# Block 0 of the first MLP in two pieces for its first two column groups: 480 tokens of five attention tiles, then the 32 of the sixth

## The chip, the cores and the metric

One core of one Trainium2 chip runs the whole program. The metric is the device time of one execution in microseconds, the median of three runs. Engines are called TensorE (PE, with its weight loads PEld), VectorE (DVE), ScalarE (ACT), GpSimd (POOL) and SyncE (SP, which here only issues transfers).

## The reference

Chunked attention over 4 batches, 8 heads, 768 positions, 64 dimensions: each chunk of 32 queries sees 8 memory positions and the keys from 16 before to 8 behind the chunk. Its output, 3072 tokens of 512, goes through two MLPs:

```python
x = attention(q, k, v, mem_k, mem_v)             # 3072 x 512
gate = 1.0 / (1.0 + np.exp(-(x @ w_gate)))       # 512 x 1536
x = gate * (x @ w_val) @ w_out                   # 1536 x 512
h = x @ w_in                                     # 512 x 2048
return (h * sigmoid(1.702 * h)) @ w_out2         # 2048 x 512
```

Weights arrive as 64-bit floats.

## The kernel before

**Tiles and blocks.** Attention is worked out in 32 tiles of 96 tokens (`TQ`), the MLPs in 6 blocks of 512 tokens (`BLK`). Block 0 is therefore tiles 0 to 4 and the first 32 tokens of tile 5; the other 64 tokens of tile 5 belong to block 1. Tiles 0 to 5 are the prologue (`NPRO` = 6) with buffers of their own; tiles 6 to 8 use one set of buffers in turn, and both kinds are transposed on PE. The tiles from 9 on are transposed on DVE, from keys and queries that SP loads in many small pieces into the buffers in which weights were converted before.

**One prologue tile** (`attention`, line 362) goes so: loads of q, k, v and memory on SP; transposes of q and k on PE (L406, L414), evicted by ACT (L421, L426, L427); scores on PE (L525); maximum and subtraction on DVE (L542, L545), exponential on ACT (L553), sum and reciprocal on DVE (L587, L589, L590); normalization on DVE and POOL (L598); transposes of the probabilities on PE (L620), evicted by ACT (L627); product with v on PE (L676); and the split of the result into a high part (ACT, L722) and a low part (DVE, L725), xh and xl, which the MLP multiplies. Tile 5's split is in two pieces, one for each block; the second, `evict(1)`, is held back and also needs the key `x1`: the buffers of block 1's xh and xl serve first as raw buffers for the weights value 1 and out 0.

**Banks.** PSUM has 8 banks: G, V, A0, A1 and Y0 to Y3. All prologue tiles use Y0 and Y1 for transposed q and k, A0 and A1 for scores, Y2 and Y3 for transposed probabilities, and G for the product with v. In the first MLP G and V take the gate and value products, Y0 to Y3 the output product.

**Weights** are turned from 64 bits into a high and a low part in 36 conversions, in the order gate 0, value 0, gate 1, value 1, out 0, gate 2, value 2, out 1, gate 3, ... (number = column group of 128 of the 1536). Each is a load on SP (L268), then on ACT L272, on DVE L277, a sign step on DVE (L286) or ACT (L282) in turn, a join on DVE (L291), the high part on ACT (L296), and the low part (L301) on DVE for two of three, on POOL for the third. From the ninth conversion on they need buffers, and from the tenth slots, of a pool that opens (`open_late`) when the prologue's buffers are given back, the last by tile 5.

**First MLP** (lines 1019 to 1038). For each block and each of the 12 column groups: the gate product (`first_product`: eight multiplies with the weight's high part, L784, four with its low part, L791), tanh on ACT (L808), the value product, the gating tail (DVE L811, ACT L816, DVE L819), and then the output product `gemm2` of the column group before (twelve multiplies, L975). `SPLIT` already cuts block 1 into two halves of 256 tokens for its first ten column groups.

**The order.** Every step is a task with an engine, an estimated duration and a due time. `Schedule.run` hands due times back from products to what they need, and then gives each engine, whenever it is free in the plan, the task with the earliest due time among those that are ready in the plan. The order of each engine is thus fixed when the program is built, and the engine follows it, whatever comes late. The products' due times come from a running `clock` that begins at 34 and adds 1.12 times each product's estimate. A prologue tile's last split is due at 34 less 2 us for each tile that comes after it among the six.

When PE would be idle before the first product, the plan puts in multiplies with an identity (`sch.fill`, L848) that write bank V.

Of the kernel before, what the change touches and what calls it, by code (L numbers as in the profile page):

```python
# [22 lines left out]
TQ = CH * NCK  # L23
# [100 lines left out]
def c_dve(n, k=1):  # L124
    return k * 0.13 + n / 960.0


def c_act(n):
    return 0.13 + n / 1200.0
# [7 lines left out]
def kernel(  # L137
# [30 lines left out]
    BLK = 512  # L168
# [4 lines left out]
    NPRO = len(tiles[0])  # L173
# [4 lines left out]
    clock = [34.0]  # L178
# [9 lines left out]
    G, V, A0, A1 = 0, 1, 2, 3  # L188
    Y = [4, 5, 6, 7]
# [129 lines left out]
    def dma(dst, src, key, r=(), act=False, dur=0.45):  # L319
        n = 8  # L320
        for d in src.shape:
            n *= d
        q_ = nc.scalar if act else nc.sync
        add("act" if act else "sp", dur, lambda: q_.dma_start(out=dst(), in_=src), r=list(r), w=[key], nbytes=n)
# [30 lines left out]
    STEP = 2.0  # L355
# [6 lines left out]
    def attention(t, bufs, banks, pe_path, extra=None, nth=0, last=False):  # L362
# [9 lines left out]
        def tadd(eng, dur, fn, r=(), w=(), more=0.0, **kw):  # L372
            add(eng, dur, fn, r=r, w=w, slack=SL + more, **kw)
# [310 lines left out]
        def evict(part=None):  # L684

            g = range(t * NCK, (t + 1) * NCK)
            for i, blk in enumerate(sorted({c // NCH for c in g})):
                if part not in (None, i):
                    continue
                cs = [c for c in g if c // NCH == blk]  # L690
                a = (cs[0] - g[0]) * CH
                m = len(cs) * CH
                x0 = cs[0] % NCH * CH
                xb = blk % 2
                if blk >= NB - 2:
                    for bk, kb, c0, p0, n in outs:
                        src = bk[:, c0 : c0 + n * TQ].rearrange("p (a s) -> p a s", a=n)[:, :, a : a + m]
                        dst = T["qt"][:, p0 : p0 + n, :m]
                        tadd("act", c_act(n * m), lambda d=dst, s=src: nc.scalar.activation(d, s, AF.Copy), r=[kb], w=[kk["qt"]])
                    o = (blk - NB + 2) * BLK + x0  # L700
                    dma(
                        lambda o=o, m=m: x_dram.rearrange("(a p) c -> p a c", p=P)[:, :, o : o + m],
                        T["qt"][:, :, :m],
                        ("xd", blk, t),
                        r=[kk["qt"]],
                        act=True,
                    )
                    continue
                due = None
                if t < NPRO and blk == 0:  # L710
                    due = clock[0] - STEP * (NPRO - 1 - t)
                elif t < NPE and blk <= 1 and SPREAD:

                    due = clock[0] + SPREAD * (t - NPRO + 1) / (NPE - NPRO)
                for o, (bk, kb, c0, p0, n) in enumerate(outs):
                    src = bk[:, c0 : c0 + n * TQ].rearrange("p (a s) -> p a s", a=n)[:, :, a : a + m]
                    at = (slice(None), slice(p0, p0 + n), slice(x0, x0 + m))
                    wx = [("x", xb, c % NCH, e) for c in cs for e in (range(2) if pe_path else (o,))]
                    rx = [kb] + (["x1"] if xb else [])

                    def ev_xh(src=src, at=at, xb=xb):
                        nc.scalar.activation(xhs[xb][at], src, AF.Copy)  # L722

                    def ev_xl(src=src, at=at, xb=xb):
                        nc.vector.tensor_tensor(  # L725
                            out=xls[xb][at], in0=src, in1=xhs[xb][at].bitcast(F32), op=ALU.subtract
                        )

                    tadd("act", c_act(n * m), ev_xh, r=rx, w=wx)
                    tadd("dve", c_dve(n * m), ev_xl, r=rx, w=wx, due=due)  # L730

        rp = kvn + [(kk["pt"], 0), (kk["pt"], 1)]
        if pe_path:
            tadd("pe", 0.8, pe_pv, r=rp, w=[kbv], margin=mg)
            if t < NPRO - 1 or t >= NPRO:
                evict()
            else:

                evict(0)
                held_back.append(lambda: evict(1))  # L740
        else:
            late.append(dict(pv=pe_pv, rp=rp, evict=evict, rest=rest))
            if last:
                for x in list(late):
                    if x is not late[0]:
                        x["rest"]()
                    tadd("pe", 0.9, x["pv"], r=x["rp"], w=[kb0, kb1])
                    x["evict"]()
                late.clear()
# [94 lines left out]
    pro = pro_stack.enter_context(tc.tile_pool(name="pro", bufs=1))  # L844
    ident = {"pro": pro.tile([P, P], F32, tag="ident", name="ident")}
    make_identity(nc, ident["pro"])
    pro_banks = [(Y[0], Y[1], A0, A1, Y[2], Y[3], G)] * NPRO
    sch.fill = lambda: nc.tensor.matmul(bank[V][:, :P], ident["pro"], ident["pro"], start=True, stop=True)  # L848
    pro_bufs = []
    for i in range(NPRO):  # L850
# [163 lines left out]
    TT = BLK // P  # L1014

    LOAD = 1.12
    SPLIT = {1: (10, BLK//2)}
    pend = None
    for b in range(NB - 2):
        n = BLK  # L1020
# [4 lines left out]
        steps = [(f, 0, n) for f in range(F1)]  # L1025
        if b in SPLIT:
            lead, c1 = SPLIT[b]
            steps[:lead] = [(f, c, m) for c, m in ((0, c1), (c1, n - c1)) for f in range(lead)]
# [538 lines left out]
```

## Time and profile before

| | before |
|---|---|
| median of 3 runs | 1166.68 us (1166.3 to 1166.88) |
| profiled execution | 1167.84 us, of it the span 1166.0 us |
| PE busy | 1150.3 us (99%) |
| DVE busy | 770.5 us (66%) |
| ACT busy | 531.1 us (46%) |
| mean granted clock of PE | 0.997 |

The span runs from the first to the last instruction of the profiled execution; its own time has 1.84 us more around it. Busy time of PE is no measure of its pace, because multiplies overlap each other; the starts of neighbouring multiplies show the pace. In rows in order of time the first column is the start, the second how long the row lasts, and what stands in brackets is the idle time ahead of it and what ended that. `x4` is four instructions in one row.

### The profile page before, as it was taken

What the parts mean: (1) busy time and instruction counts of PE and PEld (TensorE: products, weight loads), DVE (VectorE), ACT (ScalarE), POOL (GpSimd) and SP (SyncE); (2) the same over time, 40 slices, a digit from 0 to 9 for tenths busy, and PEclk for the clock granted to TensorE, in tenths of its full rate; (3) what the DMA queues carried; (4) which work ended last, traced back from release to release, by engine and by line L of the source; (5) the groups of instructions that cost most, each with busy time, mean ns of one, the idle gap of its engine ahead of it and who ended that gap; (6) DMA issues with size and microseconds to landing.
All of it is one profiled execution on the core that took longest, in us unless ns stands there. A gap on an engine that the chain in (4) does not pass through costs nothing.

```text
span 1166.0 us, 19472 instructions
## 1 busy us (share of the span) xinstructions
PE 1150.3 (99%) x7288; PEld 959.8 (82%) x7288; DVE 770.5 (66%) x1460; ACT 531.1 (46%) x953; POOL 129.1 (11%) x150
## 2 busy tenths in 40 slices
PE   8899999999999999999999999999999999999998
PEld 7788899987888888888888878888888888888886
DVE  7899657877677777888866978867244365343332
ACT  6778622223222323676545766655243353233332
POOL 5333233112222111000000001000000000000000
PEclk9899999999999999999999999999999999999999
DMA  9756244234444524344327645574233452244001
GB/s 215 218 183 198 76 106 99 51 82 115 86 95 89 118 55 119 111 169 154 108 65 225 212 166 187 174 251 123 69 121 114 126 163 82 84 123 120 27 37 36
DMA packets 211070, 144.40 MB, mean 124 GB/s; under 512 B 146208, under 2 KB 166944, under 8 KB 210976
## 3 DMA queue, kind: packets, MB, share of 16 engines
q1 hardware_dynamic: 177048, 128.74, 39.0%
q10 hardware_dynamic: 33928, 14.42, 4.5%
q8 instruction: 57, 0.93, 0.4%
q14 instruction: 37, 0.30, 0.1%
HBM read 107.45 MB, written 35.65 MB: 123 GB/s over the span
## 4 chain that ended last, share of the span: by engine, by line
PE 96%; DVE 2%; ACT 1%; DMA 0%; POOL 0%; issue 0%; SPq 0%; DVEq 0%; POOLq 0%
PE bank L1321 29%; PE bank L758 22%; PE bank L975 17%; PE bank L784 15%; PE bank L791 8%; PE bank L676 2%; PE bank L525 2%; DVE pw L598 0%; DVE sm L587 0%; DMA qn<-in_q_dram 0%; DVE e L545 0%; DVE mx L542 0%; DVE xl L725 0%; PE bank L620 0%; PE bank L414 0%; DMA vn<-in_v_dram 0%
## 5 line engine op out<-in xcount | busy, mean ns | idle before, releaser
L1321 PE MATMUL bank<-sb_x,sb_r 128*128 128x512 f32 x1512 | 362.5, 389 | 0.4 <-ACT sb_s L1333 0.4
L1321 PEld LDWEIGHTS bank<-sb_x,sb_r 128*128 128x128 f32 x1512 | 283.7, 188 | 60.0 <-ACT sb_s L1333 1.1
L758 PE MATMUL bank<-w,gh 128*128 128x512 f32 x624 | 192.1, 389 | 0.0
L784 PE MATMUL bank<-xh,w 128*128 128x512 f32 (+1 forms) x464 | 160.7, 358 | 2.7 <-DVE xl L725 1.4
L784 PE MATMUL bank<-xl,w 128*128 128x512 f32 (+1 forms) x464 | 159.5, 355 | 0.5 <-DVE xl L725 0.5
L975 PE MATMUL bank<-gh,w 128*128 128x512 f32 (+1 forms) x656 | 157.3, 365 | 0.0
L758 PEld LDWEIGHTS bank<-w,gh 128*128 128x128 f32 x624 | 117.2, 188 | 24.2
L975 PEld LDWEIGHTS bank<-gh,w 128*128 128x128 f32 x656 | 114.6, 189 | 20.1 <-ACT gh L1348 0.3
L758 PE MATMUL bank<-w,gl 128*128 128x512 f32 x312 | 121.4, 389 | 0.0
L1337 DVE TENSOR_TENSOR sb_s<-bank,sb_s 128x512 f32<-128x512 f32 x108 | 74.3, 690 | 70.6 <-PE bank L1321 58.7
L791 PE MATMUL bank<-xh,w 128*128 128x512 f32 (+1 forms) x464 | 107.5, 356 | 0.0
L1333 ACT ACTIVATE sb_s<-bank 128x512 f32<-128x512 f32 x108 | 65.0, 602 | 84.3 <-PE bank L1321 78.7
L784 PEld LDWEIGHTS bank<-xh,w 128*128 128x128 f32 x464 | 88.4, 190 | 16.5 <-ACT sig L808 2.0
L784 PEld LDWEIGHTS bank<-xl,w 128*128 128x128 f32 x464 | 88.5, 191 | 13.1 <-DVE xl L725 1.0
L791 PEld LDWEIGHTS bank<-xh,w 128*128 128x128 f32 x464 | 78.1, 189 | 12.7
L642 DVE STREAM_TRANSPOSE pt<-raw 32x256 f32<-32x256 f32 x184 | 79.7, 433 | 5.0 <-PE bank L676 1.9
L975 PE MATMUL bank<-gl,w 128*128 128x512 f32 (+1 forms) x328 | 80.3, 367 | 0.0
L808 ACT ACTIVATE sig<-bank 128x512 f32<-128x512 f32 (+1 forms) x58 | 30.6, 528 | 89.6 <-PE bank L791 79.8
L1364 ACT ACTIVATE sig<-sb_s 128x512 f32<-128x512 f32 x72 | 45.4, 632 | 57.0 <-DVE sb_s L1337 36.0
L758 PEld LDWEIGHTS bank<-w,gl 128*128 128x128 f32 x312 | 58.6, 188 | 12.3
L301 POOL TENSOR_TENSOR w<-f,w 128x512 fp32r<-128x512 f32 x17 | 27.3, 1603 | 355.4 <-ACT w L296 355.3
L816 ACT ACTIVATE gh<-sig 128x512 fp32r<-128x512 f32 (+1 forms) x58 | 32.4, 558 | 73.2 <-DVE sig L811 69.1
(161 smaller groups left out, 1494.0 us busy)
## 6 DMA issues: line engine op xcount, KB each, us to landing
sb_r<-wc_dram SPq DMA_DIRECT2D x133, 256.0 KB
raw<-in_moe_w_out_dram SPq DMA_DIRECT2D x24, 512.0 KB
raw<-in_moe_w_in_dram SPq DMA_DIRECT2D x16, 512.0 KB
wc_dram<-sb_r SPq DMA_DIRECT2D x15, 512.0 KB
wf_dram<-f SPq DMA_DIRECT2D x24, 256.0 KB
y_dram<-f ACTq DMA_DIRECT2D x24, 256.0 KB
raw<-wf_dram SPq DMA_DIRECT2D x24, 256.0 KB
out_dram<-f SPq DMA_DIRECT2D x23, 256.0 KB
```

The source lines that it names most:

```text
L301: eng.tensor_tensor(out=w[:, 1, :], in0=ft, in1=w[:, 0, :].bitcast(F32), op=ALU.subtract)
L642: nc.vector.transpose(T["pt"][r * CH : (r + 1) * CH, :, c * CH : (c + 1) * CH], T["pn"][c * CH : (c + 1) * CH, :, kb * CH : (kb + 1) * CH],)
L758: nc.tensor.matmul(ps_out, a, c, start=(first and i == 0 and j == 0), stop=(last and i == n - 1 and j == 2),)
L784: nc.tensor.matmul(bank[bk][:, :n], w[:, 0, ts[t]], x[xb][:, t, c0 : c0 + n], start=t == 0 and x is xhs, stop=False)
L791: nc.tensor.matmul(bank[bk][:, :n], w[:, 1, ts[t]], xhs[xb][:, t, c0 : c0 + n], start=False, stop=t == NK - 1)
L808: nc.scalar.activation(sig[:, :n], bank[src_sig][:, :n], AF.Tanh, scale=scale / 2)
L816: nc.scalar.activation(gh[:, :n], sig[:, :n], AF.Copy, scale=0.5)
L975: nc.tensor.matmul(bank[into[m]][:, c0 : c0 + n], w[:, wi, m * P : (m + 1) * P], g[:, :n], start=f == 0 and j == 0 and c0 == 0, stop=f == ...
L1321: nc.tensor.matmul(bank[bk], w[:, o : o + P], xt[x, k][:, xl, :], start=first and k == 0 and wl == 0 and xl == 0, stop=k == 1 and wl == 1, ...
L1333: add("act", c_act(BLK), lambda: nc.scalar.activation(work[n], bank[bk], AF.Copy), r=[("bank", bk)], w=[n])
L1337: nc.vector.tensor_tensor(out=work[n], in0=bank[bk], in1=work[n], op=ALU.add)
L1364: add("act", c_act(BLK), lambda: nc.scalar.activation(sigs[i], src(), AF.Tanh, scale=0.851), r=[ksrc], w=[ks])
```

## The change

The first two column groups of block 0 are multiplied in two pieces, with columns 0 to 479 first for both and then columns 480 to 511 for both; the output products of these pieces are cut in the same way. Tiles 0 to 4 are due 2 us apart with tile 4 at the start of the clock (each 2 us later than before), and tile 5 has no due time of its own any more: it has that of the first product that reads its 32 tokens, and of those that write its banks. Tile 5's product with v goes to bank A0 in place of G.

```diff
                 due = None
                 if t < NPRO and blk == 0:
-                    due = clock[0] - STEP * (NPRO - 1 - t)
+                    due = clock[0] - STEP * (NPRO - 2 - t) if t < NPRO - 1 else None
...
-    pro_banks = [(Y[0], Y[1], A0, A1, Y[2], Y[3], G)] * NPRO
+    pro_banks = [(Y[0], Y[1], A0, A1, Y[2], Y[3], G)] * (NPRO - 1) + [(Y[0], Y[1], A0, A1, Y[2], Y[3], A0)]
...
-    SPLIT = {1: (10, BLK//2)}
+    SPLIT = {0: (2, 5 * TQ), 1: (10, BLK // 2)}
```

By the plan's clock the first product that reads tile 5 is due at 47.6, after four products of 480 tokens (2.72 each) and one output product of 480 tokens (2.72).

## Rows read from the trace of the kernel before

**Rows 1.** Stretches: stretch, length, busy time per engine, granted clock, DMA share, GB/s

```profile
30.00:35.00 5.00, 2.76 (x33) 2.29 (x31) 5.00 (x12) 3.78 (x6) 3.50 (x2) 1.00 0.68 209
35.00:40.00 5.00, 3.55 (x31) 3.14 (x32) 4.42 (x11) 4.37 (x9) 1.49 (x3) 0.65 0.08 21
```

**Rows 2.** All engines in order of time, around the first product

```profile
34.13 0.54 DVE L725 TENSOR_TENSOR xl<-bank,xh 128x384 fp32r<-128x384 f32 x1
...
38.25 0.37 SPq L268 DMA_DIRECT2D raw_s<-in_moe_w_gate_dram  x1
...
38.74 0.62 DVE L725 TENSOR_TENSOR xl<-bank,xh 128x256 fp32r<-128x256 f32 x2 [0.27 <-ACT xh L722]
...
39.51 0.76 PE L784 MATMUL bank<-xh,w 128*128 128x512 f32 x1 [1.40 <-DVE xl L725]
...
43.44 0.40 PE L784 MATMUL bank<-xl,w 128*128 128x512 f32 x1
```

**Rows 3.** PE in order of time, at the beginning of block 2

```profile
268.30 0.50 PE L784 MATMUL bank<-xl,w 128*128 128x512 f32 x1 [0.53 <-DVE xl L725]
```

**Rows 4.** All engines in order of time, tiles 4 and 5

```profile
25.49 0.73 DVE L542 TENSOR_REDUCE mx<-bank 96x4 f32<-96x256 f32 x2
...
26.22 0.74 DVE L545 TENSOR_TENSOR e<-bank,mx 96x256 f32<-96x256 f32 x2
...
27.76 1.78 DVE L598 TENSOR_TENSOR pw<-e,sm 32x448 f32<-32x448 f32 x2
...
30.25 0.87 ACT L627 ACTIVATE pt<-bank 128x384 f32<-128x384 f32 x2 [0.41 <-PE bank L620]
...
32.98 0.47 ACT L722 ACTIVATE xh<-bank 128x384 fp32r<-128x384 f32 x1
```

**Rows 5.** DVE in order of time, the first gating

```profile
47.16 0.69 DVE L811 SCALAR_TENSOR_TENSOR sig<-sig,bank 128x512 f32<-128x512 f32 x1 [2.94 <-PE bank L791]
```

**Rows 6.** PE in order of time: tile 6, output product 0, gate 3

```profile
46.88 0.60 PE L414 MATMUL bank<-ident_a,qkn_a 128*128 128x128 f32 x4
47.23 0.48 PE L784 MATMUL bank<-xh,w 128*128 128x512 f32 x1
...
52.81 1.07 PE L975 MATMUL bank<-gh,w 128*128 128x512 f32 x4
...
64.07 0.39 PE L784 MATMUL bank<-xh,w 128*128 128x512 f32 x1
```

**Rows 7.** Groups of DVE instructions from 20 to 47 us: busy us, mean ns

```profile
L598 DVE TENSOR_TENSOR pw<-e,sm 32x448 f32<-32x448 f32 (+1 forms) x6 | 5.1, 877 | 0.0
...
L291 DVE SCALAR_TENSOR_TENSOR f<-f,raw 128x512 int32<-128x512 int32 x4 | 2.7, 673 | 0.0
L301 DVE TENSOR_TENSOR w<-f,w 128x512 fp32r<-128x512 f32 x4 | 2.7, 694 | 0.0
L587 DVE TENSOR_REDUCE sm<-e 96x8 f32<-96x512 f32 x3 | 2.0, 672 | 0.6 <-ACT e L553 0.6
L277 DVE TENSOR_SCALAR raw<-raw 128x512 int32<-128x512 int32 x4 | 1.5, 408 | 0.0
L286 DVE TENSOR_SCALAR raw<-raw 128x512 uint16<-128x512 uint16 x2 | 1.5, 741 | 0.0
```

**Rows 8.** PE in order of time: 512 columns, 256 columns, product with v

```profile
140.76 0.40 PE L784 MATMUL bank<-xh,w 128*128 128x512 f32 x1
...
142.58 0.28 PE L784 MATMUL bank<-xh,w 128*128 128x256 f32 x1
...
143.41 0.28 PE L784 MATMUL bank<-xl,w 128*128 128x256 f32 x1
143.62 0.88 PE L676 MATMUL bank<-pt,vn 128*64 128x96 f32 x16
```

**Rows 9.** Waits of DVE from 43 to 136 us: total, times, longest

```profile
DVE sig L811 <- PE bank L791: 5.1, 4, 2.9
```

**Rows 10.** ACT in order of time: the high part of gate 3

```profile
50.19 0.63 ACT L296 ACTIVATE w<-f 128x512 fp32r<-128x512 f32 x1
```

**Rows 11.** SP in order of time: the first small loads

```profile
134.16 0.80 SPq L324 DMA_DIRECT2D f<-in_q_dram  x2
```

## Prediction

> **What bounds the kernel now.** I read the stretches first, then the instructions in order of time around the first product of the first MLP, then groups and waits of VectorE (DVE), and last the place where block 2 begins. TensorE (PE) does not run well until 43.44 us: the first product starts at 39.51 and its first nine multiplies take 3.93 us, while from 43.44 on they come every 0.23 us; the stretch 35 to 40 shows a granted clock of 0.65 [rows 1, 2]. From there to the end PE is busy nearly everywhere; its waits after 140 us are few, and one of them, 0.53 us at 268.30, matters below [rows 3]. So the end moves with the moment at which PE has its stream, unless a later stage takes it back.
>
> Why 39.51? The first product reads all 512 tokens of block 0, and its bank G is also the bank in which tile 5's last product lies until both of its pieces have been split. The last low part of x is written at 38.74 (two pieces: 32 tokens of block 0 and 64 of block 1), and PE follows, while tile 4's low part is begun at 34.13 [rows 2]. The second piece waits for the buffer of x1, that is for value 1 and out 0 to be out of the raw buffers, which is why these two go through DVE before value 0 and gate 1. DVE is the engine that this stage is made of: from 30 to 35 it has no gap [rows 1], filled by tiles 3, 4, 5 and the first weights [rows 4], and its first long idle time is before 47.16, where it waits 2.9 us for PE [rows 5].
>
> **Part 1, a start without tile 5.** Between tile 3 and tile 4's normalization DVE does tile 5's two maxima and two subtractions, at 25.49 and 26.22, 1.4 us together; tile 4's normalization then starts at 27.76 and ends at 29.54 [rows 4]. With tile 5 due 13.6 us of plan later, these fall behind, and the normalization ends near 28.2. From its end to tile 4's high part of x at 32.98 it took 3.4 us (transposes, two evictions from 30.25, the product with v) [rows 4]; high and low part add about 1 us. 28.2 + 3.4 + 1.0 = 32.6: the first product can start about 7 us earlier. Its weight's low part is a DVE instruction that fits into the 3.4 us. On the queues tile 5's five loads on SyncE (SP) fall behind those of value 0 and gate 1, which so come earlier; its normalizations on GpSimd (POOL), its evictions on ScalarE (ACT) and its transposes on PE fall behind what is due for the first product, and no engine does more for it than before. Bank G is no reason to wait any more, since tile 5 now ends in A0. That bank's next user is tile 6, whose transposes there had not been needed for block 1 until long after; nothing near it waits, so I cost it at nothing, as long as tile 6 stays outside block 0.
>
> **Part 2, what the start then waits for.** PE needs four 480-token products, 48 multiplies of 0.214 us (Part 3), 10.3 us, before it comes to the first out product; that began at 52.81 before [rows 6]. But the out product writes the Y banks, through which tile 5's queries, keys and probabilities pass, so tile 5 must have left them. Its due time protects it, yet DVE has to do all of this by then, by the means of its groups [rows 7]:
> - value 0: 0.41 + 0.67 + 0.69 = 1.8; gate 1: 0.41 + 0.74 + 0.67 = 1.8; value 1: 1.8; out 0: 0.41 + 0.74 + 0.67 + 0.69 = 2.5;
> - tile 5: 0.7 + 0.7 [rows 4], sum 0.67, normalization 2 x 0.88: 3.9;
> - gating of column group 0: two of 0.69 [rows 5] = 1.4.
>
> Together 13.2 us. Between 28.2 and 32.6 DVE has some 4.4 us, of which gate 0 (0.74 + 0.67 + 0.69) and tile 4's low part (0.5) take 2.6; so 11.4 us are left at 32.6, and they end at 44.0. After tile 5's normalization come its eight transposes and two evictions, as in tile 4 about 2 us: 46.0 for the first out product, against 42.9 if PE were the limit. ACT and the weight loads have as much to do but are idle more often in these stretches, so I charge nothing for them; if a load comes late, the cover is gone and the 46.0 moves by as much. Bounds: 44.0 with no tail, 48.5 if the tail is twice as long. PE's clock before 46.0 costs nothing extra, because DVE sets that time; a lower clock would only fill the wait.
>
> **Part 3, the small pieces.** Two column groups, gate and value of 12 multiplies each: 48 pieces of 32 columns; the two out products add 24: 72 more multiplies, with as many columns in all. The trace has no such multiply. Eight of 512 columns take 1.82 us from the first's start to the next kind's (0.2275 each), and of 256 columns the first and the eighth start 0.83 us apart (0.1186) [rows 8]; the line through the two, 0.000425 a column, gives 0.024 at 32 columns, the lower end. The upper end is the shortest full-height multiply that is seen alone, a 128x128 transpose, four in 0.35 us, 0.088 each [rows 6]. In between lies the product with v, 128 rows by 96 columns: sixteen in 0.88 us with the drain of the last, 0.055 each [rows 8]. I take 0.05, the nearest in columns. 72 x 0.05 = 3.6 us after the out product's start, less 24 x 0.0136 (32 columns on that line) = 0.3 because the out products' large pieces are shorter, plus 0.35 for the transposes of tile 6 at 46.88, which lay ahead of it before and will lie behind. That is 3.6 (ends: 1.8 and 6.3). ACT and DVE get four small instructions each, beside other work: a 512-column gating takes 0.69 [rows 5], so they are cheap while these engines wait for PE.
>
> A rule weighs against this part. The Trainium skill, TensorE: Matmul & The Clock Gate, section "Wait — 56ns, not 53.3ns?", gives a floor of about 62 ns per MATMUL when its decoding is done in microcode; an estimate by it is 72 x 0.062 = 4.5 instead of 3.6, and 0.9 us more in the end. The row with 0.055 is below that floor.
>
> **The sum.** 52.81 - 46.0 = 6.8 earlier, less 3.6: 3.2 us gained. The profiled execution took 1167.84 (span 1166.0 and 1.8 around it), so 1164.6 against it; the runs' median is 1166.68, so 1163.5.
>
> **Does it last?** DVE must deliver the remaining weights 3.2 us earlier too. Up to 136 us PE never waits for a weight, while DVE waits for PE in four gatings, 5.1 us in all [rows 9]; that idle time moves out, DVE follows PE. Gate 3's high part is written at 50.19 and multiplied at 64.07: 13 us to spare [rows 6, 10]. Block 2 is the tighter point: PE stands 0.53 us there for the low part of x [rows 3], and the attention tiles of that stage hang on SP's queue of small loads, which begins at 134.16, when the converting buffers come free [rows 11], and goes on issuing up to there. If DVE finishes the weights 3 us earlier, the queue starts so much earlier.
>
> **The rivals.**
> - *Given back at block 2* (0.15): the queue of small loads does not start earlier, and PE waits at 268 for what it had won. For: the 0.53 us show that there is no spare. Against: the 5.1 us of DVE waiting for PE. Time: 1166.2 to 1167, no change.
> - *A larger gain* (0.12): DVE interleaves so well that PE is the limit, the out product at 42.9, small pieces at the lower end: 9.9 - 1.8 = 8.1, which gives 1158.6, or 1161 if half of the difference to the forecast is lost.
> - *Slower by the late pool* (0.13): buffers and identity of the next stage open when tile 5's product with v is done, by 38.25 now; the load of gate 3 goes out then and stands at the head of SP's in-order queue until then, with value 3, tile 6 and later weights behind it [rows 2]. From load to high part took 12.6 us (50.8 - 38.25), so it decides when the pool opens after 64.07 - 12.6 = 51.5; each us beyond is lost. Tile 5 put last everywhere, with POOL slow on its normalization, could reach 55: 1170. Against: the first out product needs tile 5 out of the Y banks by then.
> - *The start does not move* (0.10): PE's order is fixed beforehand; if the plan sees tile 5's probabilities ready before the first product, they stand ahead of it and PE waits for them as now, to about 38.25. Gain 1.3, small pieces 2.6 net (72 x 0.036): 1168.0.
>
> **How the numbers follow.** The forecast case has 0.50, within 1161.5 to 1165.5. A measurement here tells 0.2%, 2.3 us: faster means under 1164.35, slower over 1169.0. Of the forecast case 0.38 is faster, 0.12 within; the larger gain adds 0.12 faster, the loss at block 2 0.15 same, the late pool 0.13 slower, the unmoved start 0.06 same and 0.04 slower. Faster 0.50, same 0.33, slower 0.17. By the terms' ends the forecast case could reach 1159.7 (52.81 - 44.0 less 1.8) and 1168.7 (52.81 - 48.5 less 6.3); with the rivals the range 1160.2 to 1168.3 leaves out most of the late pool and half of the larger gain.
>
> **What would show it.** Right: first product at 31 to 34 with 480 columns; tile 5's low part of x after it; first out product near 46; 32-column multiplies spaced about 0.05; the queue of small loads starting near 131; block 2 near 265. Wrong: the first product behind tile 5's product with v; a PE wait ahead of the first out product that is not DVE's; PE waits over 1 us for gate 3 or at block 2; spacing above 0.09.

## The result, and the profile after

The kernel is slower: 1175.87 us (median of four runs, 1173.48 to 1177.34) against 1166.49, a ratio of 1.0078 (1.0058 to 1.0098). The profiled execution took 1177.34, of it the span 1175.5; the span grew by 9.5 us, and PE's records by 10.2 us of busy time (1160.5 against 1150.3). Where the 9.5 us stand can be read off places that PE passes in both traces:

| PE begins | before | after | difference |
|---|---|---|---|
| the first product | 39.51 | 35.45 | -4.06 |
| the first out product | 52.81 | 48.39 | -4.42 |
| block 1 | 142.58 | 149.73 | +7.15 |
| the second MLP | 487.42 | 497.1 | +9.7 |
| end of the span | 1166.0 | 1175.5 | +9.5 |

So part of the start is won; 11.6 us are lost between the first out product and block 1, 2.5 more before the second MLP, and nothing after that. PE in order of time in the kernel after:

```profile
35.45 0.48 PE L784 MATMUL bank<-xh,w 128*128 128x480 f32 x1 [0.57 <-DVE xl L725]
...
42.34 0.38 PE L784 MATMUL bank<-xl,w 128*128 128x480 f32 x1
43.16 0.88 PE L620 MATMUL bank<-ident,pw 96*128 96x96 f32 x8 [0.43 <-POOL pw L598]
43.82 1.11 PE L791 MATMUL bank<-xh,w 128*128 128x480 f32 x4
...
46.60 0.88 PE L676 MATMUL bank<-pt,vn 128*64 128x96 f32 x16
47.41 1.14 PE L791 MATMUL bank<-xh,w 128*128 128x480 f32 x4
...
49.25 0.18 PE L784 MATMUL bank<-xh,w 128*128 128x32 f32 x1
49.28 0.26 PE L784 MATMUL bank<-xl,w 128*128 128x32 f32 x1
...
49.95 0.26 PE L784 MATMUL bank<-xl,w 128*128 128x32 f32 x1
50.06 1.12 PE L975 MATMUL bank<-gh,w 128*128 128x480 f32 x4
...
58.42 0.60 PE L975 MATMUL bank<-gh,w 128*128 128x32 f32 x4
58.87 0.60 PE L791 MATMUL bank<-xh,w 128*128 128x32 f32 x4
59.32 0.61 PE L975 MATMUL bank<-gh,w 128*128 128x32 f32 x4
59.77 1.01 PE L975 MATMUL bank<-gl,w 128*128 128x32 f32 x4
60.62 0.77 PE L784 MATMUL bank<-xh,w 128*128 128x512 f32 x1
61.20 0.63 PE L784 MATMUL bank<-xl,w 128*128 128x512 f32 x1
...
66.31 0.52 PE L784 MATMUL bank<-xl,w 128*128 128x512 f32 x1
66.68 0.39 PE L784 MATMUL bank<-xh,w 128*128 128x512 f32 x1
...
149.73 0.28 PE L784 MATMUL bank<-xh,w 128*128 128x256 f32 x1
```

**The start.** Against the row at 39.51 of [rows 2] the first product is 4.06 earlier, 480 columns wide, and its multiplies come at full pace at once, where before the first nine took 3.93 us. Tile 5's transposes and product with v (43.16, 46.60), which stood ahead of the start before, now stand among the first four products.

**The small pieces.** From 49.28 to 49.95 six multiplies of 32 columns follow each other: 0.67 / 6 = 0.1117 us from start to start. Four take 0.45 at 58.42, at 58.87 and at 59.32, so 0.1125 each, whatever they multiply. The first of a series comes sooner (49.25 to 49.28), but the large pieces around it give that back: from 49.25 to 60.62 there are 60 small multiplies and 20 of 480 columns; 11.37 us less 20 x 0.2155 and less 0.4 for the last row, which runs at half pace, leaves 0.111 for each of the 60. An eighth of the columns of a 256-column multiply costs 0.94 of its time (0.1186, [rows 8]).

**The clock.** At 60.62 begin multiplies of 512 columns that come every 0.426 us from 61.20 to 66.31, against 0.2275 in [rows 8]: fourteen take 6.06 us in place of 3.19, and 59.77 takes 0.85 in place of 0.45, 3.3 us in all. The stretches say why (columns as in [rows 1]):

```profile
50.00:55.00 5.00, 5.00 (x33) 4.58 (x34) 2.24 (x6) 2.13 (x6) 1.29 (x1) 1.00 0.93 255
55.00:60.00 5.00, 5.00 (x41) 4.83 (x39) 2.14 (x6) 1.77 (x5) 1.27 (x1) 0.98 0.91 290
60.00:65.00 5.00, 5.00 (x14) 4.07 (x15) 3.86 (x9) 2.50 (x4) 0.00 (x0) 0.50 0.68 241
65.00:70.00 5.00, 5.00 (x26) 4.15 (x24) 0.74 (x2) 1.55 (x3) 0.00 (x0) 0.84 0.42 147
```

The granted clock is 0.50 from 60 to 65, the lower of PE's two levels, right behind the stretch of small pieces. PE shows 5.00 of 5 busy in all four rows, and its weight loads 4.83 in the second: neither figure gives the loss away, only the clock and the starts do.

**Later.** From block 1 to the second MLP PE stands still for longer: 3.2 us against 1.7, which is 1.5 of the 2.5 us lost there; the rest is not assigned. The waits of PE from 138 to 500 us in the kernel after (total, times, longest):

```profile
PE bank L784 <- DVE sig L811: 2.3, 2, 1.3
PE bank L784 <- ACT sig L808: 0.9, 2, 0.5
```

Before, they were two for `sig` (ACT) of 1.2 us and one for the low part of x of 0.5 [rows 3].

### The profile page after: what moved, and what is told of

It reads as the page before. It is cut to its first block, busy times and chain, and to the rows that moved or that the text cites. A ratio compares the mean times of both kernels' runs of the same rounds, so it can differ in the third digit from the quotient of the medians.

```text
span 1175.5 us, 19627 instructions
## 1 busy us (share of the span) xinstructions
PE 1160.5 (99%) x7358; PEld 968.7 (82%) x7358; DVE 769.5 (65%) x1464; ACT 532.3 (45%) x957; POOL 128.2 (11%) x150
## 4 chain that ended last, share of the span: by engine, by line
PE 90%; SPq 3%; DMA 2%; DVE 1%; issue 0%; POOL 0%; ACT 0%; DVEq 0%; POOLq 0%
PE bank L1321 29%; PE bank L758 22%; PE bank L975 15%; PE bank L784 13%; PE bank L791 7%; SPq L324 3%; PE bank L676 2%; PE bank L525 1%; DMA f<-in_q_dram 1%; DMA vn<-in_v_dram 1%; DMA raw<-in_k_dram 0%; PE bank L620 0%; DVE pt L642 0%; DMA wf_dram<-f 0%; POOL f L1009 0%
## 5 line engine op out<-in xcount | busy, mean ns | idle before, releaser
L784 PE MATMUL bank<-xh,w 128*128 128x512 f32 (+3 forms) x480 | 165.1, 356 | 3.8 <-DVE sig L811 2.3
L784 PE MATMUL bank<-xl,w 128*128 128x512 f32 (+3 forms) x480 | 163.7, 353 | 0.0
L975 PE MATMUL bank<-gh,w 128*128 128x512 f32 (+3 forms) x672 | 160.2, 363 | 0.0
L791 PE MATMUL bank<-xh,w 128*128 128x512 f32 (+3 forms) x480 | 109.7, 353 | 0.0
L784 PEld LDWEIGHTS bank<-xh,w 128*128 128x128 f32 x480 | 91.9, 191 | 18.6 <-DVE sig L811 3.2
L784 PEld LDWEIGHTS bank<-xl,w 128*128 128x128 f32 x480 | 91.8, 191 | 12.4 <-DVE xl L725 0.3
L791 PEld LDWEIGHTS bank<-xh,w 128*128 128x128 f32 x480 | 80.1, 189 | 12.4
L975 PE MATMUL bank<-gl,w 128*128 128x512 f32 (+3 forms) x336 | 81.9, 366 | 0.0
L816 ACT ACTIVATE gh<-sig 128x512 fp32r<-128x512 f32 (+3 forms) x60 | 32.7, 545 | 84.8 <-DVE sig L811 72.3
L808 ACT ACTIVATE sig<-bank 128x512 f32<-128x512 f32 (+3 forms) x60 | 30.8, 513 | 81.2 <-PE bank L791 70.2
L975 PEld LDWEIGHTS bank<-gl,w 128*128 128x128 f32 x336 | 58.3, 190 | 9.6
```

Source lines behind the costliest of these rows:

```text
L784: nc.tensor.matmul(bank[bk][:, :n], w[:, 0, ts[t]], x[xb][:, t, c0 : c0 + n], start=t == 0 and x is xhs, stop=False)
L791: nc.tensor.matmul(bank[bk][:, :n], w[:, 1, ts[t]], xhs[xb][:, t, c0 : c0 + n], start=False, stop=t == NK - 1)
L808: nc.scalar.activation(sig[:, :n], bank[src_sig][:, :n], AF.Tanh, scale=scale / 2)
L816: nc.scalar.activation(gh[:, :n], sig[:, :n], AF.Copy, scale=0.5)
L975: nc.tensor.matmul(bank[into[m]][:, c0 : c0 + n], w[:, wi, m * P : (m + 1) * P], g[:, :n], start=f == 0 and j == 0 and c0 == 0, stop=f == ...
```

## The experiments

A line that stands in every experiment's result: the kernel before, on the same chip, took 1166.4 to 1166.8.

**1. The bank alone.** The kernel before with tile 5's product with v in A0:

```diff
-    pro_banks = [(Y[0], Y[1], A0, A1, Y[2], Y[3], G)] * NPRO
+    pro_banks = [(Y[0], Y[1], A0, A1, Y[2], Y[3], G)] * (NPRO - 1) + [(Y[0], Y[1], A0, A1, Y[2], Y[3], A0)]
```

> The kernel before with one line of the change: tile 5's product with v goes to bank A0 in place of G; due times and pieces as before. If the wait for bank G (tile 5's second piece, behind the x1 buffer) was part of what held the first product at 39.51, it now starts at 37 to 38.5 and the time falls by 0.5 to 2 us (1164.5 to 1166.0). If the low part of tile 5's first piece holds it alone, the start stays at 39 to 39.5 and the time within 0.5 us of before.

Measured: 1166.1 (1164.7 to 1170.07, ten runs), ratio 0.9997 (0.9987 to 1.0006). The first product began at 37.53, 2.0 us earlier, with tile 5 still ahead of it, and block 1 at 139.50, 3.1 earlier. About half of the earlier start is thus the bank's: the first product no longer waits until tile 5's second piece has left G. One trace tells a start to about 1 us only: with the same order up to there it lies at 37.75 and 39.09 in runs 11 and 12, and that of the kernel before at 40.19 in run 13. The start came as the first case had said, the median as the second: it shows little of it.

**2. Bank and due times, no cut.** The change without its entry in `SPLIT`:

```diff
-    SPLIT = {0: (2, 5 * TQ), 1: (10, BLK // 2)}
+    SPLIT = {1: (10, BLK // 2)}
```

> The changed kernel without the cut of block 0: bank A0 and the later due times stay, all products have 512 columns. No 32-column multiply is left. If these are the loss, their 72 times 0.11 us and the stretch at a low clock behind them are gone, and the time is 1165 to 1168, near before. If the later due times or tile 5's place in the order are the loss (late pool, attention of block 2), it stays above 1172.

Measured: 1170.88 (1169.66 to 1172.04), ratio 1.0037 (1.0024 to 1.0049), between the two ranges. Run 1 differs from it in the due times alone and is 4.8 us faster. The profiled execution, the fastest of the six, begins the first product at 39.87, block 1 at 142.47 and the second MLP at 489.2. Against the kernel before it is level at block 1 and 1.8 us late at the second MLP. Against run 1 (37.53, 139.50, 484.54) it is 2.3, 3.0 and 4.7 us late: the later due times give the bank's gain at the start away again, and 1.7 us more are lost behind block 1, where neither small pieces nor tile 5 are at work.

**3. The cut at 384.**

```diff
-    SPLIT = {0: (2, 5 * TQ), 1: (10, BLK // 2)}
+    SPLIT = {0: (2, 384), 1: (10, BLK // 2)}
```

> The changed kernel with the cut at 384 columns in place of 480: the second pieces have 128 columns. First theory: a multiply with 128x128 weights of this type takes at least 0.11 us, whatever its columns; then the 128-column ones are also spaced 0.11 and the two pieces together cost 72 x (0.111 + 0.177 - 0.2275) = 4.4 us more than one, against 7.0 in the changed kernel; with less or no fall of the clock the time is 1167 to 1172. Second theory: narrow multiplies pay more per column (0.111 for 32 is 0.003 a column); then 128 columns are spaced 0.2 to 0.4 and the time is 1178 or more.

Measured: 1173.71 (1172.82 to 1174.24), ratio 1.0059 (1.0044 to 1.0074). PE in order of time, multiplies of 128 columns:

```profile
48.91 0.27 PE L784 MATMUL bank<-xl,w 128*128 128x128 f32 x1
49.02 0.27 PE L784 MATMUL bank<-xh,w 128*128 128x128 f32 x1
...
49.58 0.28 PE L784 MATMUL bank<-xl,w 128*128 128x128 f32 x1
```

Six steps in 0.67 us: 0.1117, to the last digit what 32 columns cost. Four times the columns change nothing, so the price does not hang on the columns. The granted clock stays at 1.00 from 50 to 70 here, and the weight loads are busy 5.00 of 5 from 50 to 55. The time lies above the first theory's 1167 to 1172: block 1 begins at 143.82, 1.2 us behind before, and 3.3 us more are lost up to the second MLP (491.96).

**4. The cut at 256, tiles 3 to 5 late.** Tiles 0 to 2 alone are due before the first product; tiles 3 to 5 use A0:

```diff
-                    due = clock[0] - STEP * (NPRO - 2 - t) if t < NPRO - 1 else None
+                    due = clock[0] - STEP * (2 - t) if t < 3 else None
...
-    pro_banks = [(Y[0], Y[1], A0, A1, Y[2], Y[3], G)] * (NPRO - 1) + [(Y[0], Y[1], A0, A1, Y[2], Y[3], A0)]
+    pro_banks = [(Y[0], Y[1], A0, A1, Y[2], Y[3], G)] * 3 + [(Y[0], Y[1], A0, A1, Y[2], Y[3], A0)] * (NPRO - 3)
...
-    SPLIT = {0: (2, 5 * TQ), 1: (10, BLK // 2)}
+    SPLIT = {0: (2, 256), 1: (10, BLK // 2)}
```

> Cut at 256 columns, so that the first pieces need tiles 0 to 2 alone: tile 2 is due at the start of the clock, tiles 3 to 5 when the second pieces are, and their products with v go to A0. 256 columns are spaced 0.119 in the trace, so the pieces cost 72 x (2 x 0.119 - 0.2275) = 0.7 us. If narrow pieces and the clock behind them are the whole loss, the clock stays full from the first product on, and an earlier start (31 to 34) is kept in part: 1161 to 1165. If DVE sets the pace of this stage whatever PE does, the first out product comes no earlier than before and the time is 1166 to 1169.

Measured: 1188.36 (1187.06 to 1189.49), ratio 1.0185. The first product began at 31.25 and the first out product at 62.03. Waits of PE from 25 to 70 us:

```profile
PE bank L620 <- POOL pw L598: 11.8, 2, 9.7
```

Three late tiles hang on POOL's normalization, and PE has nothing to do meanwhile; from 45 to 65 the clock is at 0.50. It says nothing on the price of 256 columns; run 6 does.

**5. One column group cut.**

```diff
-    SPLIT = {0: (2, 5 * TQ), 1: (10, BLK // 2)}
+    SPLIT = {0: (1, 5 * TQ), 1: (10, BLK // 2)}
```

> Only the first column group is cut at 480; 36 small multiplies instead of 72. Theory 1 (each multiply with 128x128 weights takes at least 0.111 us, however few its columns): the small pieces cost 4.0 us instead of 8.0, and the granted clock does not fall behind them, which gives back 3 us more; against it, tile 5's low part of x is needed two products (5 us) earlier, so PE may wait some 2 us for it: 1169 to 1173. Theory 2 (the loss comes from the later due time of tile 5, 4 us in the run without a cut, and not from the number of small multiplies): within 1.5 us of the change's 1175.9.

Measured: 1176.29 (1169.39 to 1177.02), ratio 1.0069 (1.0045 to 1.0092): a miss for theory 1's number, and within theory 2's 1.5 us of the change. PE in order of time:

```profile
40.26 0.88 PE L620 MATMUL bank<-ident,pw 96*128 96x96 f32 x8 [2.77 <-POOL pw L598]
40.92 0.47 PE L784 MATMUL bank<-xh,w 128*128 128x480 f32 x1
```

With 36 small multiplies the plan takes tile 5 ahead of the first product again, PE waits 2.77 us for its probabilities, and the start is at 40.92. The granted clock, which theory 1 had expected to stay up, is at 0.66 from 40 to 45, behind the wait of 2.77 us, and again from 50 to 60, behind a pause of 1.0 us and the first 16 of the 36 small multiplies. What was saved at the one place was lost at the others, so the time fits theory 2 but does not tell the theories apart.

**6. The cut at 256, the rest as in the change.**

```diff
-    SPLIT = {0: (2, 5 * TQ), 1: (10, BLK // 2)}
+    SPLIT = {0: (2, 256), 1: (10, BLK // 2)}
```

> As the change, but the cut is at 256 columns, so both pieces are 256 wide. Theory 1: multiplies of 256 columns come every 0.114 us, just above the floor of 0.111, so two of them cost what one of 512 does (0.227), the cut is free and the granted clock stays at full speed behind it: about 4 us under the run cut at 384 (1173.7), so 1169.5, with the first product at 35. Theory 2 (every piece has a price of its own, about 0.1 us, whatever its width): 72 x 0.1 = 7 us above the uncut run, 1174 to 1178.

Measured: 1172.18 (1168.99 to 1172.73), ratio 1.0042 (1.0026 to 1.0058). In the profiled execution (1168.99) the first product begins at 34.69 and block 1 at 139.55, 3.0 us ahead of before: this cut costs little (0.120 us a multiply, where 0.114 was expected; two are 0.24 against 0.2275, so 0.9 us for 72), as theory 1 has it, and a price of 0.1 per piece is out. But the time is not 1169.5. The second MLP begins at 488.48, so 4.1 us are lost behind block 1. All engines in order of time at block 2 show to what:

```profile
262.14 1.31 SPq L324 DMA_DIRECT2D f<-in_mem_k_dram  x4
263.55 8.02 SPq L324 DMA_DIRECT2D f<-in_q_dram  x12
264.92 1.30 POOL L1009 TENSOR_TENSOR f<-w 128x512 f32<-128x512 f32 x1
271.67 0.38 SPq L324 DMA_DIRECT2D wf_dram<-f  x1
273.84 0.60 ACT L995 ACTIVATE f<-bank 128x512 f32<-128x512 f32 x1 [7.70 <-DMA wf_dram<-f]
274.88 0.60 ACT L808 ACTIVATE sig<-bank 128x512 f32<-128x512 f32 x1 [0.45 <-ACT f L995]
275.53 0.50 PE L784 MATMUL bank<-xh,w 128*128 128x512 f32 x1 [3.47 <-ACT sig L808]
```

Read it from below. PE waits 3.47 us for a gate's tanh; ACT does that tanh late because its eviction of block 1's output product (L995) stood 7.70 us ahead of it; that eviction needs a staging buffer, which holds weights that `park` has put together for the second MLP; POOL's addition was done at 266.2, but the store out of the buffer is issued by SP at 271.67, behind twelve loads of queries. SP's queue begins with the small loads at 133.98, against 134.16 in [rows 11]: PE came 3 us early, the queue did not.

**7. The change with the old due times.**

```diff
-                    due = clock[0] - STEP * (NPRO - 2 - t) if t < NPRO - 1 else None
+                    due = clock[0] - STEP * (NPRO - 1 - t)
```

> The change's cut and bank with the old due times, so that tile 5 comes before the first product again. Theory 1 (the later due time costs some 4 us by itself, as in the run without a cut, and the small pieces 8 us plus the clock): the start is as in the run with the bank alone (37.5), 1166.1 + 8.0 = 1174, and up to 3 more if the clock falls; not clearly slower than the change although the first product starts 2 us later. Theory 3 (the due time pays: 2 us of start, and its 4 us are a loss only where the first product waits for tile 5): 1177.5 to 1179, 2 us or more above the change.

Measured: 1176.83 (1176.09 to 1179.13), ratio 1.0093 (1.0076 to 1.011): 1 us above the change with overlapping runs, and under theory 3's range. Theory 1 had 1174 without a fall of the clock and up to 3 more with one; the clock does not fall, so its mechanism leaves 2.8 us open. Against the bank alone (run 1) only the cut differs. From the first product to block 1 PE takes 108.7 us (38.14 to 146.80) against 102.0 (37.53 to 139.50): 6.7 us for the 72 small multiplies, where 72 x (0.111 - 0.012) gives 7.1 (0.012 is what 480 columns are cheaper than 512). Up to the second MLP (496.08) 4.2 us more are lost behind block 1. Its stretches:

```profile
55.00:60.00 5.00, 5.00 (x40) 4.77 (x39) 1.92 (x6) 2.17 (x5) 0.60 (x1) 1.00 0.34 105
60.00:65.00 5.00, 5.00 (x29) 4.29 (x29) 5.00 (x11) 3.64 (x5) 0.67 (x1) 1.00 0.32 71
```

Here the clock does not fall behind the same 72 multiplies. So the multiplies alone don't bring the fall about.

**8. The plan told the true price.** Order only:

```diff
     def c_mm(n, k):
-        return k * (n / 2400.0 + step_ns[0])
+        return k * max(n / 2400.0 + step_ns[0], 0.111 if n < 256 else 0.0)
```

> The change, with the planner told that a multiply of under 256 columns takes 0.111 us (it reckons 0.016 for 32 columns). Only the order of the work changes. Theory 4 (of the 9.4 us lost, the 2 us that appear as PE's waits for gatings between block 1 and the second MLP come from a plan whose clock runs 7 us ahead): those waits fall from 3.2 to under 2 us and the time to 1173 to 1174.5. Rival (the waits come from the order that follows from tile 5's late due time): waits and time unchanged, 1175 to 1177.

Measured: 1183.14 (1180.0 to 1184.05), ratio 1.0137. Theory 4 falls, and the rival's "unchanged" too. Block 1 begins at 145.79, 3.9 us ahead of the change (the clock is 1.00 from 35 to 80), the second MLP at 502.8, 5.7 behind it. One of its waits, PE in order of time:

```profile
408.77 0.50 PE L784 MATMUL bank<-xh,w 128*128 128x512 f32 x1 [4.45 <-ACT sig L808]
```

Ahead of it ACT's eviction L995 waited 4.4 us, to 403.36, for the store of parked weights, which is the mechanism of run 6 at another output product; the next eviction then stood 2.5 us, to 407.64, behind loads of v that ACT itself issues. A better estimate made a worse order.

**9 to 12. The store off SP's queue.** `park`'s store issued by ACT (runs 9 and 11) or by POOL, right behind its own addition (runs 10 and 12), on the cut at 256 of run 6 (runs 9 and 10) and on the bank alone of run 1 (runs 11 and 12):

```diff
-        dma(lambda: wf_dram[slot], st, ("wf", slot), r=[kst])
+        def store():
+            nc.gpsimd.dma_start(out=wf_dram[slot], in_=st)
+
+        add("pool", 1.0, store, r=[kst], w=[("wf", slot)], nbytes=P * 512 * 4)
```

(with ACT: the same `dma` call with `act=True, dur=0.1`).

> The cut at 256 with the store of the parked weights (out of the staging buffers) issued by ACT instead of SP. Theory 5 (the cut at 256 reaches block 1 three us early and loses it because SP's in-order queue starts no earlier: the store that frees a staging buffer stands behind twelve loads of queries, ACT's eviction of the out product waits 7.7 us for it, and PE 3.5 us for the gating behind that eviction): the 3.5 us wait at block 2 goes, SP has some 0.4 us less to issue per store, and the time falls from 1172.2 to 1168 to 1169.5. Rival (the attention tiles of block 2 hang on the loads themselves, so that PE waits for the low part of x instead): the wait changes its name, 1171 to 1173.

> The same with the store issued by POOL, right behind its own addition. Theory 5: as before, 1168 to 1169.5. Rival: 1171 to 1173, or more if POOL's issuing holds its normalizations up.

> The bank of tile 5 alone (1166.1 before) with the store of the parked weights issued by ACT. Theory 5: the first product starts 2 us early there as well and block 2 is where some of it goes; with the store off SP's queue 1164 to 1165.5. Rival: unchanged, 1165.5 to 1166.7.

> The bank of tile 5 alone with the store of the parked weights issued by POOL. Theory 5: 1164 to 1165.5. Rival: unchanged, 1165.5 to 1166.7, or more if POOL's issuing holds its normalizations up.

| run | store by | base | us | ratio to before |
|---|---|---|---|---|
| 9 | ACT | cut at 256 | 1164.8 (1163.93 to 1165.72) | 0.9981 (0.9971 to 0.9991) |
| 10 | POOL | cut at 256 | 1163.53 (1163.0 to 1164.8) | 0.9968 (0.9956 to 0.9979) |
| 11 | ACT | bank alone | 1164.5 (1163.67 to 1169.34) | 0.9992 (0.9979 to 1.0005) |
| 12 | POOL | bank alone | 1163.91 (1162.31 to 1164.9) | 0.9969 (0.9958 to 0.9981) |

The cut at 256 gains 8.7 us by it (1172.18 to 1163.53), more than theory 5 had said; runs 11 and 12 lie in its range or just under it, and the interval of run 11 holds 1. All engines in order of time in run 10:

```profile
254.03 1.30 SPq L324 DMA_DIRECT2D f<-in_mem_k_dram  x4
255.44 12.53 SPq L324 DMA_DIRECT2D f<-in_q_dram  x24
...
261.03 1.30 POOL L1009 TENSOR_TENSOR f<-w 128x512 f32<-128x512 f32 x1
262.74 0.58 POOL L1013 DMA_DIRECT2D wf_dram<-f  x1 [0.41 <-POOL f L1009]
...
266.94 0.60 ACT L995 ACTIVATE f<-bank 128x512 f32<-128x512 f32 x1 [4.58 <-DMA wf_dram<-f]
```

The store goes out 0.4 us after the addition, the eviction is 6.9 us earlier (266.94 against 273.84), and SP's queue itself is 8.1 us further (254.03 against 262.14). Up to there SP issues 225 loads in both runs, from 133.98 and 133.96 on, in run 6 with eleven stores among them. The stores take 5.3 us of the 8.1 (0.4 each to issue and 0.1 ahead of it); the queue's other waits are 4.1 us longer in run 6, one of them 2.9 us for a load of v at 192.58; and the issuing of the loads is 1.2 us shorter. None of the eleven waits for POOL's addition: in run 6 the store is late because it stands behind loads. In other orders a store does hold the queue, in run 2 for 5.0 us, up to 149.31, until POOL's addition is done, and in the kernel before for 2.2 us, up to 148. Each of these edits also makes the plan anew, so that the gains contain another order of the engines.

**13 to 15. The same store on the other kernels:** the kernel before, the change, and the change without a cut (run 2), each with the diff of run 10.

> The kernel before with nothing changed but the store of the parked weights, issued by POOL. Theory 5 (SP's queue binds at block 2 only when PE arrives there early; before, PE waited 0.5 us there): 1165.5 to 1166.8, so that what the bank and the cut at 256 gain is the earlier start. Rival (SP's queue binds in every one of these kernels): 1163.2 to 1164.6, the same as with the bank or the cut, which are then worth nothing by themselves.

> The change itself with the store of the parked weights issued by POOL. Theory 1 with theory 5: what remains against the cut at 256 with the same store (1163.5) is the floor of the 72 small multiplies, 72 x (0.111 + 0.215 - 0.227) = 7.1 us, and up to 3 where the granted clock falls: 1170.5 to 1173.7. Rival (the late waits of the change have another cause than SP's queue): 1175 to 1177, unchanged.

> The change's due times and bank without a cut (1170.9 before), with the store of the parked weights issued by POOL. Theory 5: the 4 us that the due times cost by themselves were a matter of SP's queue and go, 1166 to 1167.5. Rival (they come from the order in which DVE and ACT do tile 5's work before the first product, which is 0.4 us later): 1169.5 to 1171.

| kernel | store by SP | store by POOL | gain |
|---|---|---|---|
| before | 1166.74 | 1164.87 (1163.14 to 1165.94) | 1.9 |
| bank alone | 1166.1 | 1163.91 | 2.2 |
| the change without a cut | 1170.88 | 1164.92 (1164.08 to 1166.32) | 6.0 |
| the change, cut at 256 | 1172.18 | 1163.53 | 8.7 |
| the change, cut at 480 | 1175.87 | 1172.05 (1169.45 to 1173.48) | 3.8 |

Before gains 1.9 us, between the two theories: its waits behind block 1 (1.7 us) are gone from the trace. Of the 4.8 us that the due times cost against the bank alone, 1.0 is left with POOL's store (1164.92 against 1163.91), and 1164.92 is level with the kernel before's 1164.87: most of that cost hung on this store. And run 14 against run 15, which differ in the cut alone, gives what the cut does by itself: 1172.05 - 1164.92 = 7.1 us lost, with the earlier start (34.68 against 39.59) and a fall of the clock (0.67 from 60 to 65 in run 14) counted in. Run 14 lies where theory 1 with theory 5 had put it; run 15 is better than theory 5 had said.

## Why the prediction was wrong

**What held.** The first product starts without tile 5, 480 columns wide, and the first out product is earlier, by 4.42 us of the 6.8 forecast. The late pool does not decide: the load of gate 3 goes out at 47.62, ahead of the 51.5 of that rival, and PE never waits for gate 3. DVE follows PE: its waits for PE up to block 1 grow from 5.1 us [rows 9] to 14.3, and PE waits for no weight.

**Part 1, the start: 32.6 forecast, 35.45 measured.** Tile 4's normalization ended as forecast (POOL's part at 28.16, against 28.2), and its transposes begin at 28.22. From there I counted tile 4's own steps alone. All engines in order of time:

```profile
28.22 0.88 PE L620 MATMUL bank<-ident,pw 96*128 96x96 f32 x8 [1.69 <-ACT kt L427]
...
28.80 0.87 ACT L627 ACTIVATE pt<-bank 128x384 f32<-128x384 f32 x2
...
31.85 0.42 DVE L542 TENSOR_REDUCE mx<-bank 96x4 f32<-96x256 f32 x1 [0.65 <-PE bank L525]
32.19 0.54 DVE L725 TENSOR_TENSOR xl<-bank,xh 128x384 fp32r<-128x384 f32 x1
32.66 0.41 DVE L542 TENSOR_REDUCE mx<-bank 96x4 f32<-96x256 f32 x1
...
32.91 0.88 PE L676 MATMUL bank<-pt,vn 128*64 128x96 f32 x16
32.99 0.74 DVE L545 TENSOR_TENSOR e<-bank,mx 96x256 f32<-96x256 f32 x2
...
34.25 0.68 DVE L291 SCALAR_TENSOR_TENSOR f<-f,raw 128x512 int32<-128x512 int32 x1
...
34.85 0.55 DVE L725 TENSOR_TENSOR xl<-bank,xh 128x384 fp32r<-128x384 f32 x1
```

Tile 4's probabilities are evicted by 29.67, but its product with v begins only at 32.91. It writes bank G, as those of tiles 0 to 3 do, and tile 3's low part (32.19) is the last to read G before it. In run 14, which has the same order here, PE waits for just that: the row at 32.01 has [0.29 <-DVE xl L725]. So "Bank G is no reason to wait any more" held for tile 5 alone. Nor was tile 5's work gone from DVE: its first maximum stands ahead of tile 3's low part and waits 0.65 us for tile 5's scores, and its subtraction and a weight's join stand ahead of tile 4's low part, which begins at 34.85, 0.7 us later than in [rows 2]. A task without an early due time is put in wherever its engine would be free in the plan. The start came earlier because it no longer waits for tile 5's end and for tile 5's pieces in bank G.

**Part 2, the first out product: 46.0 forecast by DVE, 48.39 measured, set by PE.** From 35.45 PE has 48 multiplies of 0.2155 (10.3), tile 5's eight transposes and its product with v (0.66 + 0.81, from each start to the next kind's) and a pause ahead of the transposes (0.82 from 42.34 to 43.16, less the multiply's 0.2155: 0.6): 12.4 of the 12.94 us. I had costed tile 5's work on PE at nothing, as if DVE covered it. And "PE's clock before 46.0 costs nothing extra" missed what was there to win: the half pace of the first nine multiplies, 1.9 us [rows 2].

**Part 3, the small pieces: this is the step that failed.** Sized at 0.05 each with the upper end 0.088, they take 0.111. In the part's own sum that is 72 x 0.111 - 0.3 + 0.35 = 8.0 us in place of 3.6, and above the upper end of 6.3; against uncut products, whose pieces of 480 come sooner too, it is 72 x (0.111 - 0.012) = 7.1. I priced them by columns, from a line through 512 and 256 [rows 8]. Down to 256 columns the columns set the pace; below, something else does, at 0.111 for 32 and for 128 columns of tokens alike.

Neither of the rows beside that line was a step from start to start. The upper end came from the four transposes at 46.88 [rows 6], 0.35 us up to the next kind. But the multiply behind them begins 0.03 us after the last of them; the fourth begins 0.325 us after the first, so the step is 0.108, and 72 x 0.108 = 7.8. Their group, with the first and the last start:

```profile
L414 PE MATMUL bank<-ident_a,qkn_a x4: 270/272/272, 46.9 to 47.2; 128*128 128x128 f32 x4
```

The product with v, at 0.055, was the length of a row with its drain over sixteen. Its single starts in the trace come in pairs, 0.007 us apart, with one pair every 0.083; its weights have 64 columns (`128*64`), half as many. My own test, "spacing above 0.09", was the right one.

What sets the 0.111 is argued, not shown. It fits the loading of the weights, a new load of 128 rows and 128 columns before each multiply, because the loads' own rows have the same step (PEld in order of time, kernel after):

```profile
49.26 0.19 PEld L784 LDWEIGHTS bank<-xl,w 128*128 128x128 f32 x1
49.36 0.19 PEld L784 LDWEIGHTS bank<-xh,w 128*128 128x128 f32 x1
...
49.92 0.19 PEld L784 LDWEIGHTS bank<-xl,w 128*128 128x128 f32 x1
```

Six in 0.66 us from 49.26 on. The Trainium skill, TensorE: Matmul & The Clock Gate, section "LDWEIGHTS (loading the stationary operand)", says that a load's time grows with the columns of the weights and not with their rows, and gives P / 1.2 ns for P columns; an estimate by it is 128 / 1.2 = 107 ns, and the 111 here is near it. The transposes of tile 5's probabilities at 43.16 do not fit it: their loads have 96 rows and the same 128 columns and come every 0.083 us, so there the measurement decides. No run changes the form of the weights alone. I had weighed the issue floor of another section, 62 ns, which no row here shows to bind.

**A missing term: the clock behind the small pieces, 3.3 us.** The sum had none. To block 1 the account reads: start -4.06, first multiplies at full pace -1.9, tile 5's work on PE and the pause behind the start +2.1, small pieces +7.1, clock +3.3, together +6.5 of the 7.15 measured; 0.6 is not assigned. Run 7, with the same cut but tile 5 ahead of the start and no fall of the clock, bears two of them out: it takes 5.6 us less from the first product to block 1 (108.7 against 114.3), where 2.1 + 3.3 = 5.4. The fall of the clock is seen, its cause is not settled: it came again in runs 14 and 5, with the same small multiplies it did not come in runs 7 and 8, and the change's four runs, at mean clocks of 0.996 to 0.998, lie 3.9 us apart, the fastest with the highest clock.

**Does it last? No.** "Given back at block 2" was priced as a loss of the gain at most, 1166.2 to 1167, and its condition is what the runs at 256 show: PE arrives 3 us early, the small loads begin at 133.98, and PE waits. But it can cost more than was won. In the change itself PE comes late and SP's queue with it (small loads from 146.19), and still 2.5 us more are lost up to the second MLP. With POOL's store the change gains 3.8, the same kernel uncut 6.0. That the order behind block 1 shifts with every edit ahead of it, by up to 8.7 us through this one store, was in none of my cases; I had read the 0.53 us of [rows 3] as a place without slack, and not asked what held it.

## What to carry to other kernels

Cutting a multiply along its tokens is nearly free only as long as each piece stays above the shortest step of such multiplies: here 256 columns cost 0.120 us, and 128 or 32 cost 0.111 with weights of 128 x 128, so 480 and 32 cost 1.4 times what 512 do, while 256 and 256 cost 1.05 times. Before an operation that the trace does not show is priced by the nearest row, compare both operands with that row's, not only the one that changes, and take the step between starts inside a series, not its length over its count. And a store of an engine's result, whose buffer another engine waits for, does not belong on an in-order queue among loads that others wait for: moved to POOL, which makes the data, it took 1.9 us off the kernel before (1164.87, ratio 0.9985, 0.9976 to 0.9995), and with the cut at 256 the time fell to 1163.53 (0.9968, 0.9956 to 0.9979), the fastest median here, level with the bank alone at 1163.91.

## What was not expected of the hardware

The granted clock fell to 0.50 while the profile had PE busy without a gap, behind a stretch of multiplies of 32 columns (the change and run 14), and did not fall behind the same 72 multiplies in two other orders (runs 7 and 8). A multiply of 32 columns and one of 128 cost the same 0.1117 us, with weights of 128 x 128. Two multiplies with weights of 64 columns began 0.007 us apart, and such a pair came every 0.083 us. Issuing the store took POOL 0.58 us of its time, and it went out 0.41 us after the addition.
